# Seven half-width products for the first output block, and new places for v, the rounding, the audit and the flag's product, in a one-core attention and MLP kernel

## Chip, cores and metric

One core of a Trainium2 chip. The time is the device time of one launch in microseconds (us), the median of several runs; every number called a span, a start or a wait is from a profiled execution. All runs named here were in the fast state. Engines: PE is TensorE's matmuls, PEld its weight loads, DVE VectorE, ACT ScalarE, POOL GpSimd, SP the engine that issues the DMAs.

## The reference

```python
def _attn_ref(q, k, v, alpha):                 # each (4, 8, 768, 48) float32
    state = np.zeros((B, H, D, D), dtype=np.float32)
    for t in range(S):
        state = alpha[:, :, t, :, None] * state + np.einsum('bhd,bhe->bhde', k[:, :, t], v[:, :, t])
        y[:, :, t] = np.einsum('bhd,bhde->bhe', q[:, :, t], state)
    return y

def _moe_ref(x, w_in, w_out):                  # x (3072, 384), w_in (384, 2048), w_out (2048, 384)
    h = x @ w_in
    g = h * (1.0 / (1.0 + np.exp(-h)))
    return (g @ w_out).astype(np.float32)
# reference: x is the attention's y, with the heads beside each other
```

The weights arrive as 64-bit floats, so the kernel itself rounds them to 32 bits.

## The kernel before

The sequence is cut into 24 chunks of 128 tokens (six times four batches). A chunk passes through four stages: `products` (transposes of alpha, k, q, then scans on DVE that scale k and q into `kp` and `qp`), `scores` (k times q, masked into `g`), `values` (`g` times `v`, plus the state) and `states`. The program gives the name `g` to the MLP's middle values too: a `g` in front of the values products is the masked scores, a `g` in front of input pieces or output products is a block of the MLP. Between the stages PE is filled with *pieces* of the MLP: input pieces (`enter_plain`, `enter`) and output products (`leave`). Weight pieces come by DMA as 64-bit words into a short ring (`fetch`) and are rounded by one ACT instruction on the low words and three on DVE (`weights`).

Two things besides the result matter here. Most output products use a scheme of seven half-size products in place of eight (`leave`, with sums and differences of blocks of `w_out` formed in `differences`); the first half group alone still multiplied plainly. And an *audit* reads alpha and both weight matrices once more, a piece at a time, takes their extremes on DVE, and sends the verdict through one tiny matmul, the *flag's product*; if it fails, a general path runs instead.

```python
    load(0)
    load(1)
    for _ in range(4):
        fetch()                        # four 512 KB weight pieces are queued first
    ...
    for n in range(NV):
        load_v(n)                      # only then v of the first two chunks
    ...
    def weights(which):
        ...
        for dst, src in pieces:
            ...
            bits = coming.pop(0)
            lo, hi = bits.bitcast(U32)[:, :, 0], bits[:, :, 1]
            up = upp.tile([128, 512], I32, name="up")[:, 0:n]
            tc.keep_in_program_order(act.activation(up, lo, AF.Copy, scale=2.0**-29))
            ...                        # three DVE instructions: shift, sign, add
            fetch()
            yield
    ...
    def leave(grp, h):
        ...
        if grp == h == 0:              # the first half group: plain, 384 columns wide
            halves = w_out.rearrange("p (i k) n -> p k i n", k=2)
            ps = [out_bank(m, HD) for m in range(2)]
            for j in range(HF // 2):
                for m in range(2):
                    for i in (2 * j, 2 * j + 1):
                        for e in range(2):
                            ...
                            pe.matmul(ps[m], lhsT=x, rhs=halves[:, e, i], ...)
            ...
            return
        ...                            # all the others: seven products of 192 columns
    ...
    def fill(step, slot):
        ...
        if at % 2 == 0 and step > 3 * GB:
            next(audits, None)         # one audit item: DMA now, reduction at the next call
    ...
    turns = 0
    while next(audits, 0) is None:     # the tail: the rest of the audit between products
        turns += 1
        for _ in range(1 + turns % 2):
            go_on()
    ...
    go_on()
    go_on()
    ps = ps_attn()[0:1, 0, 0:1]
    pe.matmul(ps, lhsT=good, rhs=mask[:, 0, C - 1 : C], start=True, stop=True)   # the flag's product
```

Of the kernel before, what the change touches and what calls it, by code (L numbers as in the profile page):

```python
# [9 lines left out]
I32 = mybir.dt.int32  # L10
# [345 lines left out]
def quotients(  # L356
# [135 lines left out]
    def fetch():  # L492

        if wide and sources:
            src = sources.pop(0)
            n = src.shape[1]
            bits = raw.tile([128, 512, 2], I32, name="bits")[:, 0:n, :]
            nc.sync.dma_start(bits.rearrange("p n w -> p (n w)"), src.bitcast(I32))
            coming.append(bits)

    load(0)
    load(1)
    for _ in range(4):
        fetch()



# [46 lines left out]

        return quads[:, at // NKT, at % NKT] if at < 4 * NKT else late["wx"][:, at - 4 * NKT]

    for n in range(NV):
        load_v(n)

    def combine(to, sa, a, sb, b):  # L560
        if sa == sb == 1:
# [18 lines left out]
    def differences(i):  # L580

        if i < HF // 2:
            i = slice(2 * i, 2 * i + 2)
            tc.keep_in_program_order(
                dve.tensor_tensor(t1[:, i], b12[:, i], b11[:, i], ALU.subtract))
            dve.tensor_tensor(t2[:, i], b22[:, i], t1[:, i], ALU.subtract)
            dve.tensor_tensor(t4[:, i], b21[:, i], t2[:, i], ALU.subtract)
        else:
            i -= HF // 2
            if i % 2 == 0:  # L590
                side_by_side(0, 1, i // 2)
            i = slice(2 * i, 2 * i + 2)
            dve.tensor_tensor(b12[:, i], b22[:, i], b12[:, i], ALU.subtract)

    def weights(which):




        pieces = [  # L600
            (w_in[:, t, c : c + 512], moe_w_in[t * 128 : t * 128 + 128, c : c + 512])
            for t, c in pieces_in
        ] if which == 0 else [
            (w_out[:, f, :], moe_w_out[f * 128 : f * 128 + 128, :]) for f in range(NFT)]
        for dst, src in pieces:
            if not wide:
                act.dma_start(dst, src)
                yield
                continue
            n = dst.shape[1]  # L610
            bits = coming.pop(0)
            assert which == 0 or conv_done[0] == n_conv[0]
            lo, hi = bits.bitcast(U32)[:, :, 0], bits[:, :, 1]
            up = upp.tile([128, 512], I32, name="up")[:, 0:n]

            tc.keep_in_program_order(act.activation(up, lo, AF.Copy, scale=2.0**-29))
            w = dst.bitcast(I32)
            tc.keep_in_program_order(
                dve.tensor_scalar(w, hi, 3, 0x3FFFFFFF, ALU.logical_shift_left, ALU.bitwise_and))
            dve.scalar_tensor_tensor(w, hi, -(1 << 30), w, ALU.bitwise_and, ALU.bitwise_or)  # L620
            dve.tensor_tensor(w, w, up, ALU.add)  # L621
            fetch()
            yield

# [218 lines left out]
    def enter_plain(grp, h, pair):  # L843

        if h == 0:
            g_tiles(grp, pair)
        xt = xts[2 * grp + h]
        for f in range(8 * pair, 8 * pair + 8, 2):
            ps = bank(f // 2 % 3).rearrange("p (e n) -> p e n", e=2)
            for e in range(2):  # L850
                for t in range(NKT):
                    pe.matmul(ps[:, e, :], lhsT=w_in[:, t, (f + e) * 128 : (f + e + 1) * 128],  # L852
                              rhs=xt[:, t, :], start=(t == 0), stop=(t == NKT - 1))
            q, i = divmod(f, 4)
            act.activation(gts[grp, h, pair][:, i : i + 2, q % 2, :], ps, AF.Silu)  # L855
            if grp == 1 and pair == 0:
                differences(4 * h + f // 2)
            if grp > 0 and f % 8 == 6:
                side_by_side(grp, h, pair)
            yield  # L860
# [105 lines left out]
    def leave(grp, h):  # L966


        def product(ps, m, k, w, first=False):
            for i in range(HF):  # L970
                q = i // 2
                x = gts[grp, h, q // 2][:, 2 * (i % 2) + k, q % 2, m * C : (m + 1) * C]
                pe.matmul(ps, lhsT=x, rhs=w[:, i], start=(first and i == 0), stop=(i == HF - 1),  # L973
                          skip_group_check=True)

        def subtract(to, x, y):
            for pair in range(NQ // 2):
                dve.tensor_tensor(cells(grp, h, pair, *to), cells(grp, h, pair, *x),  # L978
                                  cells(grp, h, pair, *y), ALU.subtract)

        def store(m, c, x, y=None):
            ci, b = divmod(GB * grp + 2 * h + m, B)
            o = opool.tile([128, HO], F32, name="o")
            if y is None:
                act.copy(o, x)
            else:
                dve.tensor_tensor(o, x, y, ALU.add)
            r = b * S + ci * C
            nc.sync.dma_start(out[r : r + C, c * HO : (c + 1) * HO], o)

        if grp == h == 0:

            halves = w_out.rearrange("p (i k) n -> p k i n", k=2)
            ps = [out_bank(m, HD) for m in range(2)]
            for j in range(HF // 2):
                for m in range(2):
                    for i in (2 * j, 2 * j + 1):
                        for e in range(2):
                            x = gts[grp, h, j // 2][:, 2 * (i % 2) + e, j % 2, m * C : (m + 1) * C]
                            pe.matmul(ps[m], lhsT=x, rhs=halves[:, e, i],  # L1000
                                      start=(i == e == 0), stop=(i == HF - 1 and e == 1),
                                      skip_group_check=True)
                if j < HF // 2 - 1:
                    yield
            for m in range(2):
                for c in range(2):
                    store(m, c, ps[m][:, c * HO : (c + 1) * HO])
            yield
            return

        u1, u2, u3, u4 = [rpool.tile([128, HO], F32, name=f"u{j}") for j in range(4)]
        steps = iter(range(7))

        def done():
            if 2 * grp + h in (1, 2):
                sums_w(2 * grp + h - 1, 4 * next(steps) + 4)

        def new(i):
            return out_bank(i, HO)

        a, b = new(0), new(1)
        product(a, 0, 0, b11, True)
        act.copy(u1, a)
        subtract((0, 0), (1, 0), (0, 0))
        done()
        yield
        product(b, 1, 0, t1, True)
        act.copy(u4, b)
        done()
        yield  # L1030
        product(a, 0, 1, b21)
        store(0, 0, a)
        subtract((0, 1), (0, 1), (0, 0))
        done()
        yield
        b = new(1)
        product(b, 0, 0, t2, True)
        dve.tensor_tensor(u2, b, u1, ALU.add)
        subtract((1, 0), (1, 1), (0, 0))
        dve.tensor_tensor(u2, u2, u4, ALU.add)  # L1040
        done()
        yield
        a = new(0)
        product(a, 0, 1, b22, True)
        store(0, 1, a, u2)
        done()
        yield
        product(b, 1, 0, b12)
        dve.tensor_tensor(u3, b, u1, ALU.add)
        store(1, 1, u3, u4)  # L1050
        done()
        yield
        a = new(0)
        product(a, 1, 1, t4, True)
        store(1, 0, a, u3)
        done()
        yield
# [27 lines left out]
    for h in range(2):  # L1085
        for pair in range(2):
            pieces += [plain(0, h, pair)] * 4
    pieces += [(leave(0, 0), 24, GB)] * (HF // 2)
    phases = [len(pieces)]
    for h in range(2):  # L1090
        pieces += [plain(1, h, 0)] * 4
    both([(leave(0, 1), 12, GB)] * 7, [plain(1, 0, 1)] * 4 + [plain(1, 1, 1)] * 4)
    phases.append(len(pieces))
    before = output(1)
# [35 lines left out]
    def fill(step, slot):  # L1130

        at = step * SLOTS + slot
        if at < marks[0]:
            if step >= 1:
                convert(0, (at - SLOTS) * 3 // (marks[0] - SLOTS) + 1)
            return
        i = next(i for i, m in enumerate(marks[1:]) if at < m)
        a, b = [work_at[n] for n in ([0] + phases)[i : i + 2]]
        due = a + (b - a) * (at - marks[i] + 1) / (marks[i + 1] - marks[i])
        if at % 2 == 0 and step > 3 * GB:  # L1140
            next(audits, None)
        while work_at[done + 1] <= due and pieces[done][2] <= bridged:
            convert(0, 3 * (done // 2) + 6)
            convert(1, 3 * (done - 6) // 2)
            go_on()
# [42 lines left out]
        dve.tensor_single_scalar(e, e, bound, holds)  # L1188
    good = work.tile([128, 1], F32, name="good")
    dve.tensor_reduce(good, ends, axis=AX, op=ALU.min)  # L1190
    go_on()
    go_on()
    ps = ps_attn()[0:1, 0, 0:1]
    pe.matmul(ps, lhsT=good, rhs=mask[:, 0, C - 1 : C], start=True, stop=True)
    dve.tensor_single_scalar(small, ps, 127.5, ALU.is_ge)
# [62 lines left out]
```

## Time and profile before

| | kernel before |
|---|---|
| median time | 569.04 us (568.75 to 571.14, 3 runs) |
| span of the profiled execution | 567.3 us |
| PE busy | 549.0 us, 97% |
| DVE busy | 445.0 us, 78% |
| PE idle in front of the first values / near 232 us / at the flag's product | 2.4 / 1.8 / 2.1 us |

PE is busy for nearly the whole span, so the share of the other engines says little; what counts is the short list of PE's own waits. The prediction shows those lines and how they are read.

### The profile page before, as it was taken

How to read it: one execution, taken by the hardware profiler on the slowest of the kernel's cores; microseconds unless marked ns; L12 is line 12 of the kernel's file. 1: busy time of each engine (PE TensorE's matmuls, PEld its weight loads, DVE VectorE, ACT ScalarE, POOL GpSimd, SP SyncE). 2: the span in 40 equal slices, each digit the busy share in tenths (PEclk: the TensorE clock that was granted, in tenths of full speed). 3: DMA queues.
4: the chain of work that ended last, by engine and by line, in shares of the span. 5: the costliest groups of instructions: out<-in, count | busy, mean ns of one | idle time of the engine just before them, and what ended most of it. 6: DMA issues, size and time to landing. Idle time of an engine off the chain costs nothing.

```text
span 567.3 us, 12315 instructions
## 1 busy us (share of the span) xinstructions
PE 549.0 (97%) x5026; PEld 489.4 (86%) x5026; DVE 445.0 (78%) x815; ACT 205.4 (36%) x407; POOL 14.6 (3%) x36
## 2 busy tenths in 40 slices
PE   6899999999999999899999999999999999998996
PEld 4777887678999999799989999998999999997995
DVE  5797898488898599996998897999995866746531
ACT  3555543134323342443433443434443241421200
POOL 4111000100000000000000000000000000000000
PEclk9999999999999999999999999999999999998999
DMA  9989981533243324444425544425431223331000
GB/s 229 205 242 221 217 191 36 136 103 82 70 113 100 83 64 108 126 130 111 132 69 159 143 111 127 135 75 157 127 97 44 66 69 99 92 116 44 14 29 25
DMA packets 94415, 63.78 MB, mean 112 GB/s; under 512 B 55312, under 2 KB 86032, under 8 KB 94352
## 3 DMA queue, kind: packets, MB, share of 16 engines
q1 hardware_dynamic: 94352, 62.94, 43.1%
q8 instruction: 40, 0.66, 0.5%
q14 instruction: 23, 0.19, 0.1%
HBM read 58.20 MB, written 4.72 MB: 111 GB/s over the span
## 4 chain that ended last, share of the span: by engine, by line
PE 69%; DVE 17%; DMA 9%; SPq 2%; issue 1%; ACT 1%; DVEq 0%; ACTq 0%
PE ps_o L973 25%; PE ps_m L875 15%; PE ps_m L852 13%; DMA bits<-in_moe_w_out_dram 6%; PE ps_a L794 6%; PE ps_o L1000 4%; DVE seen L657 3%; PE ps_a L751 3%; DVE turn L668 1%; DMA vn<-in_v_dram 1%; PE ps_a L768 1%; DVE g L889 1%; DVE g L978 1%; DVE p L722 1%; PE ps_a L688 1%
## 5 line engine op out<-in xcount | busy, mean ns | idle before, releaser
L973 PE MATMUL ps_o<-w_out,g 128*128 128x192 f32 x704 | 122.4, 328 | 0.0
L973 PEld LDWEIGHTS ps_o<-w_out,g 128*128 128x128 f32 x704 | 115.3, 190 | 2.3 <-issue 0.4
L973 PE MATMUL ps_o<-wt,g 128*128 128x192 f32 x528 | 92.0, 328 | 0.0
L852 PE MATMUL ps_m<-xt,w_in 128*128 128x256 f32 x384 | 89.2, 383 | 1.3 <-DVE w_in L621 0.7
L973 PEld LDWEIGHTS ps_o<-wt,g 128*128 128x128 f32 x528 | 88.2, 192 | 1.4
L852 PEld LDWEIGHTS ps_m<-xt,w_in 128*128 128x128 f32 x384 | 70.9, 190 | 11.9 <-DVE w_in L621 1.6
L875 PE MATMUL ps_m<-xc,w_in 128*128 128x256 f32 x288 | 70.1, 379 | 1.4 <-DVE g L889 1.4
L875 PEld LDWEIGHTS ps_m<-xc,w_in 128*128 128x128 f32 x288 | 54.0, 190 | 7.9 <-DVE g L889 1.7
L886 ACT ACTIVATE g<-g 128x1024 f32<-128x1024 f32 x32 | 33.0, 1054 | 59.1 <-DVE g L889 59.1
L657 DVE TENSOR_REDUCE seen<-bits 128x1 f32<-128x384 int32 (+2 forms) x65 | 42.4, 687 | 15.1 <-DMA bits<-in_moe_w_out_dram 14.9
L875 PE MATMUL ps_m<-xc,wx 128*128 128x256 f32 x192 | 50.4, 384 | 0.0
L881 ACT COPY g<-ps_m 128x512 f32<-128x512 f32 x64 | 36.8, 586 | 36.2 <-PE ps_m L875 36.2
L978 DVE TENSOR_TENSOR g<-g 128x512 f32<-128x512 f32 x66 | 44.4, 683 | 7.0 <-PE ps_o L973 7.0
L774 ACT ACTIVATE st<-st,least 128x96 f32<-128x96 f32 x80 | 24.0, 365 | 59.1 <-DVE least L696 59.1
L889 DVE TENSOR_TENSOR g<-ps_m,g 128x512 f32<-128x512 f32 x56 | 37.1, 680 | 2.3 <-PE ps_m L875 2.1
L875 PEld LDWEIGHTS ps_m<-xc,wx 128*128 128x128 f32 x192 | 34.9, 190 | 4.2 <-issue 0.4
L693 DVE TENSOR_TENSOR_SCAN u<-al,one 128x516 f32<-128x516 f32 x24 | 29.0, 1209 | 9.0 <-ACT al L690 8.9
L855 ACT ACTIVATE g<-ps_m 128x512 f32<-128x512 f32 x32 | 19.1, 596 | 41.8 <-PE ps_m L852 41.6
L722 DVE TENSOR_TENSOR_SCAN p<-al,inv 128x516 f32<-128x516 f32 x24 | 29.4, 1227 | 5.0 <-PE ps_a L794 4.7
L762 DVE TENSOR_TENSOR g<-ps_a,mask 128x512 f32<-128x512 f32 x40 | 25.7, 684 | 9.0 <-PE ps_a L751 8.7
L794 PE MATMUL ps_a<-g,vn 128*32 128x128 f32 x768 | 27.2, 282 | 2.4 <-DMA vn<-in_v_dram 2.4
L794 PEld LDWEIGHTS ps_a<-g,vn 128*32 128x32 f32 x768 | 20.3, 112 | 10.1 <-issue 8.4
(127 smaller groups left out, 654.7 us busy)
## 6 DMA issues: line engine op xcount, KB each, us to landing
bits<-in_moe_w_in_dram SPq DMA_DIRECT2D x24, 512.0 KB, 4.7
bits<-in_moe_w_out_dram SPq DMA_DIRECT2D x32, 384.0 KB, 3.3
at<-in_alpha_dram SPq DMA_DIRECT2D x64, 96.0 KB, 2.3
kt<-in_k_dram SPq DMA_DIRECT2D x64, 96.0 KB, 2.4
qt<-in_q_dram SPq DMA_DIRECT2D x64, 96.0 KB, 2.5
bits<-in_alpha_dram SPq DMA_DIRECT2D x9, 512.0 KB, 3.6
out_dram<-o SPq DMA_DIRECT2D x48, 96.0 KB, 1.7
an<-in_alpha_dram SPq DMA_DIRECT2D x8, 192.0 KB, 5.1
```

The source lines that it names most:

```text
L657: dve.tensor_reduce(seen[kind][which][:, i : i + 1], x, axis=AX, op=op, apply_absolute_value=True))
L693: dve.tensor_tensor_scan(u[:, end - 1 :: -1], sg[:, end:0:-1], one[:, end:0:-1], 0.0, ALU.mult, ALU.add)
L722: dve.tensor_tensor_scan(p[:, 0:end], sg[:, 0:end], iv[:, 0:end], 0.0, ALU.mult, ALU.add)
L762: dve.tensor_tensor(g[:, u].rearrange("p (o j) c -> p o j c", o=2), ps[u].rearrange("p (o j) c -> p o j c", o=2), m.to_broadcast([128, 2, ...
L794: pe.matmul(py[32 * at : 32 * at + 32, t, :], lhsT=w, rhs=x, start=(i < 4), stop=(i >= len(todo) - 4), skip_group_check=True)
L852: pe.matmul(ps[:, e, :], lhsT=w_in[:, t, (f + e) * 128 : (f + e + 1) * 128], rhs=xt[:, t, :], start=(t == 0), stop=(t == NKT - 1))
L875: pe.matmul(ps[:, e], lhsT=block_w(w)[:, 2 * pair + e], rhs=block_x(grp, x), start=(first and e == 0), stop=(e == 1), skip_group_check=True)
L881: act.copy(to, ps)
L886: act.activation(x, x, AF.Silu)
L889: dve.tensor_tensor(to, a, b, op)
L973: pe.matmul(ps, lhsT=x, rhs=w[:, i], start=(first and i == 0), stop=(i == HF - 1), skip_group_check=True)
L978: dve.tensor_tensor(cells(grp, h, pair, *to), cells(grp, h, pair, *x), cells(grp, h, pair, *y), ALU.subtract)
```

## The change

Intent: save columns on PE (seven products of 192 columns for the last plain block), and take away three PE waits (for v at the start, for DVE near 232 us, for the audit's verdict near the end). The line numbers of the changed kernel differ by a few from those of the kernel before: values L794 becomes L800, input pieces L852 and L875 become L858 and L882, output products L973 become L980, the flag's product L1194 becomes L1180.

```diff
-    for _ in range(4):
+    for i in range(4):
         fetch()
+        if i % 2 == 0:
+            load_v(i // 2)
...
-    for n in range(NV):
-        load_v(n)
...
-            tc.keep_in_program_order(act.activation(up, lo, AF.Copy, scale=2.0**-29))
+            up = ahead.pop() if ahead else rounding(bits)
...
             dve.tensor_tensor(w, w, up, ALU.add)
+            if i + 1 < len(pieces):
+                ahead.append(rounding(coming[0]))
...
-            if grp == 1 and pair == 0:
-                differences(4 * h + f // 2)
+            if grp == 1 and pair == h == 0:
+                differences(f // 2)
+                differences(4 + f // 2)
...
-        if grp == h == 0:
-            ...                        # the plain product, removed
...
-    pieces += [(leave(0, 0), 24, GB)] * (HF // 2)
+    pieces += [plain(1, 0, 0)] * 4 + [(leave(0, 0), 12, GB)] * 7
     phases = [len(pieces)]
-    for h in range(2):
-        pieces += [plain(1, h, 0)] * 4
+    pieces += [plain(1, 1, 0)] * 4
...
-        if at % 2 == 0 and step > 3 * GB:
+        if at % 2 == 0 and step > 3 * GB + 2:
             next(audits, None)
...
-    go_on()
-    go_on()
+    for _ in range(5):
+        go_on()
     ps = ps_attn()[0:1, 0, 0:1]
     pe.matmul(ps, lhsT=good, rhs=mask[:, 0, C - 1 : C], start=True, stop=True)
```

More of the change, by code (lines that the diff above doesn't have):

```diff
@@ L589, in differences @@
             i -= HF // 2
-            if i % 2 == 0:
-                side_by_side(0, 1, i // 2)
+            side_by_side(0, i % 2, i // 2)
             i = slice(2 * i, 2 * i + 2)
@@ L604, in weights, with rounding @@
             (w_out[:, f, :], moe_w_out[f * 128 : f * 128 + 128, :]) for f in range(NFT)]
-        for dst, src in pieces:
+        def rounding(bits):
+            n = bits.shape[1]
+            up = upp.tile([128, 512], I32, name="up")[:, 0:n]
+            tc.keep_in_program_order(
+                act.activation(up, bits.bitcast(U32)[:, :, 0], AF.Copy, scale=2.0**-29))
+            return up
+        ahead = []
+        for i, (dst, src) in enumerate(pieces):
             if not wide:
@@ L609, in weights @@
                 continue
-            n = dst.shape[1]
+            assert which == 0 or conv_done[0] == n_conv[0]
             bits = coming.pop(0)
-            assert which == 0 or conv_done[0] == n_conv[0]
-            lo, hi = bits.bitcast(U32)[:, :, 0], bits[:, :, 1]
-            up = upp.tile([128, 512], I32, name="up")[:, 0:n]
-            tc.keep_in_program_order(act.activation(up, lo, AF.Copy, scale=2.0**-29))
-            w = dst.bitcast(I32)
+            up = ahead.pop() if ahead else rounding(bits)
+            hi, w = bits[:, :, 1], dst.bitcast(I32)
             tc.keep_in_program_order(
@@ L989, in store @@
             nc.sync.dma_start(out[r : r + C, c * HO : (c + 1) * HO], o)
-        if grp == h == 0:
-            halves = w_out.rearrange("p (i k) n -> p k i n", k=2)
-            ps = [out_bank(m, HD) for m in range(2)]
-            for j in range(HF // 2):
-                for m in range(2):
-                    for i in (2 * j, 2 * j + 1):
-                        for e in range(2):
-                            x = gts[grp, h, j // 2][:, 2 * (i % 2) + e, j % 2, m * C : (m + 1) * C]
-                            pe.matmul(ps[m], lhsT=x, rhs=halves[:, e, i],
-                                      start=(i == e == 0), stop=(i == HF - 1 and e == 1),
-                                      skip_group_check=True)
-                if j < HF // 2 - 1:
-                    yield
-            for m in range(2):
-                for c in range(2):
-                    store(m, c, ps[m][:, c * HO : (c + 1) * HO])
-            yield
-            return
         u1, u2, u3, u4 = [rpool.tile([128, HO], F32, name=f"u{j}") for j in range(4)]
```

## The prediction

> **What bounds the kernel now.** I read the page first (busy time, then the 40 slices), then the list of waits with TensorE as the one that waits, then the timeline around each wait, and last the chain that ended last, for rates.
>
> The page and the waits of TensorE:
> ```profile
> PE 549.0 (97%) x5026; PEld 489.4 (86%) x5026; DVE 445.0 (78%) x815; ACT 205.4 (36%) x407; POOL 14.6 (3%) x36
> ...
> PE ps_a L688 <- DMA an<-in_alpha_dram: 4.2, 1, 4.2
> PE ps_a L794 <- DMA vn<-in_v_dram: 2.4, 1, 2.4
> PE ps_a L1194 <- DVE good L1190: 2.1, 1, 2.1
> PE ps_m L875 <- DVE g L889: 1.8, 2, 1.4
> PE ps_m L852 <- DVE w_in L621: 0.7, 1, 0.7
> ```
> TensorE (PE) is the bound. Of the 567.3 us span it is idle 18.3 us, and about 5.5 us of those are the wait for the last store after its last product, 4.2 us the first load. So only two things can make the kernel faster: fewer columns through PE, or removal of a wait in that short list. Each has its part of the change. The rates that I need, from the chain that ended last (start, length, number of instructions):
> ```profile
> 111.15 5.16 PE ps_o L1000 x16
> 145.18 2.60 PE ps_o L973 x16
> ```
> A matmul in the code is two instructions here (32 in the code, 64 in the group of L1000). A 384-column instruction costs 5.16 / 16 = 0.3225 us, a 192-column one 2.60 / 16 = 0.1625 us: in proportion to the columns, no fixed cost to speak of.
>
> The flag's product, in the timeline of PE, and just before it the last audit reduction on VectorE (DVE):
> ```profile
> 515.20 1.01 DVE L657 TENSOR_REDUCE seen<-bits 128x1 f32<-128x384 int32 x2 [1.17 <-DMA bits<-in_moe_w_out_dram]
> ...
> 516.87 0.19 PE L1194 MATMUL ps_a<-mask,good 128*1 128x1 f32 x2 [2.11 <-DVE good L1190]
> ...
> 518.43 1.91 PE L875 MATMUL ps_m<-xt,w_in 128*128 128x256 f32 x4
> 520.13 3.56 PE L973 MATMUL ps_o<-wt,g 128*128 128x192 f32 x16
> 523.53 1.03 PE L875 MATMUL ps_m<-xc,w_in 128*128 128x256 f32 x4
> ```
> PE waits 2.1 us for the audit's end, and then runs slowly: four instructions take 1.91 us where the same four take 1.03 later. The windows view agrees: granted clock 0.92 in 510 to 520 us and 0.91 in 520 to 530, so about 0.8 + 0.9 = 1.7 us of full speed are lost after the wait itself.
>
> The start, in the timelines of PE, POOL and DVE:
> ```profile
> 16.53 1.94 PE L794 MATMUL ps_a<-g,vn 128*32 128x128 f32 x32 [2.41 <-DMA vn<-in_v_dram]
> ...
> 13.76 1.40 POOL L758 TENSOR_SCALAR_AFFINE_SELECT g<-g 128x512 f32<-128x512 f32 x2 [6.75 <-ACT g L757]
> ...
> 19.61 0.69 DVE L621 CUSTOM_DVE_ANT_0 w_in<-w_in,up 128x1024 uint16<-128x1024 uint16 x1 [2.01 <-ACT up L616]
> ...
> 22.93 0.69 DVE L621 CUSTOM_DVE_ANT_0 w_in<-w_in,up 128x1024 uint16<-128x1024 uint16 x1 [1.56 <-ACT up L616]
> ```
> v of the first chunk is issued at 8.55 us behind four weight pieces and lands 7.85 us later. But g, the other operand, is ready only at 14.5 (first half) and 15.2 us. DVE twice waits for ScalarE (ACT) to have rounded the low words, 3.6 us in all.
>
> The middle, in the timelines of DVE and PE:
> ```profile
> 218.34 1.22 DVE L657 TENSOR_REDUCE seen<-bits 128x1 f32<-128x1024 f32 x1
> ...
> 229.07 1.21 DVE L657 TENSOR_REDUCE seen<-bits 128x1 f32<-128x1024 f32 x1
> ...
> 233.73 1.13 PE L875 MATMUL ps_m<-xc,w_in 128*128 128x256 f32 x4 [1.37 <-DVE g L889]
> ```
> From 200 to 235 us DVE is 97% busy, the first two audit reductions stand in its queue, and PE then waits for it: 1.4 + 0.4 us.
>
> [...]
>
> **The change part by part.**
> 1. The product of the first half group by seven products. Removed: 64 instructions of 384 columns, 64 x 0.3225 = 20.6 us. Added: 7 x 8 matmuls of 192 columns, 112 instructions, 112 x 0.1625 = 18.2 us. PE gains 2.4 us. DVE gets six subtractions (0.68 us each) and five small sums (0.36 us), and the differences of w_out (16 of 0.55 us) come before this stage, not at 120 to 131 us. To make room, one block of four input pieces is moved ahead of it. DVE was busy 18.6 us of 88 to 118, so there is room. By the instruction order, w_out's last rounding and all differences precede these products on DVE. Adding durations along it from the sixth chunk's scan (about 84 us), DVE has rounded everything at about 95 us and formed all differences at about 102; PE, which now has 10.4 us of input pieces first, wants the first at about 100 and needs t1 at about 104. No wait, by 2 us at the tightest. Gain 2.4.
> 2. v sooner. v now stands behind one weight piece, so by bytes it lands near 12 to 13 us (an estimate: the first piece landed at 11.22 and the next 1.7 MB took 5.2 us). Then g decides. Here part 3 gives something back: the rounding of the second piece now stands ahead of the copies of g in ACT's queue, that piece lands at about 13.3 us (same estimate), so g comes at about 15.3 to 16.0. PE starts its values about 1 us sooner instead of 2.4[...].
> 3. Rounding one piece ahead. DVE's waits of 2.0 and 1.6 us mostly go; what PE sees of it is the 0.7 us wait for w_in and less crowding up to 50 us. [...]Parts 2 and 3 together: 1.3 us.
> 4. Audit two steps later. The two reductions before 233 us (2.4 us of DVE) go, more than the 1.8 us wait. Expect 1.5 us, as another order may bring part back.
> 5. The flag. In the new instruction order PE has about 34 blocks of 2.6 us (16 instructions) between its last attention product and the flag's, 88 us; before about 25, 65 us. The audit has 18 items left there; before, the last 14 items came every 4.5 us (450.9 to 516.1, with DMA, reduction and one buffer in a ring). 17 x 4.5 = 77 us plus 1.5. The flag is ready some 8 us early: 2.1 us of wait and 1.7 us of half clock go, 3.8 us. I count 3.4 for the risk. Eight blocks, 21 us, remain after the flag, enough to hide its reading.
>
> Sum: 2.4 + 1.3 + 1.5 + 3.4 = 8.6 us. The time of the runs is 569.04, so about **560.4 us**.
>
> **Rivals.** (a) ACT becomes the wait: [...]a rounding put ahead now waits for its DMA or for DVE in front of copies and Silus that PE needs. For it: ACT already waited 5.9 us for pieces and 4.3 us for DVE at L616. Against: PE has three banks there and was idle under 2 us from 20 to 100 us. If it holds, parts 2 and 3 give nothing: 562. (b) The audit's chain paces the tail. The last subtractions of the second-last output stand behind its last reductions on DVE; PE needs them about 83 us after its last attention product, the chain ends at 77 to 79. At 5 us an item the flag wait turns into a wait of a product: 563 to 564. (c) DVE becomes the bound where the differences now stand (60 to 105 us, it was 83 to 95% busy to 90 us): each us late is a us of PE, perhaps 2: 562. (d) All goes as hoped, the start gives its full 2.4 and DVE's lead frees PE from 20 to 50 us too: 12 us, 557.
>
> **Range and chances.** Parts 1 and 5 are nearly sure in size, 6 us; parts 2 to 4 hold 0 to 6. So 557.3 to 563.6. Two per cent is 11.4 us, to 557.7, and wants every part in full: 0.10. Slower by two per cent needs a new wait of 20 us that nothing in the order suggests: 0.01. Within: 0.89.
>
> **What would show it.** Right: no L1000-type group, 112 more instructions of 192 columns; no PE wait for the flag's product and granted clock 1.00 to the end of PE; no PE wait on DVE near 230 us; the wait at the first values shorter and put to POOL or ACT and not to DMA. Wrong: a new PE wait on w_out, wt or Silu between 80 and 110 us (part 1, rival c or a), a PE wait on the subtractions in the last 60 us (rival b), or gaps elsewhere from a scheduler's order that I did not foresee.

## The result

563.48 us (563.20 to 564.50, 4 runs) against 569.69 (568.75 to 571.14, 4 runs in all) for the kernel before: ratio 0.9892, 95% interval 0.9865 to 0.9919, within two per cent. A ratio here is the mean time of one kernel's fast runs over that of the other's of the same rounds, so it is not quite the ratio of the medians quoted. The span fell from 567.3 to 561.6 us.

The busy times of the changed kernel's page:
```profile
PE 543.9 (97%) x5074; PEld 492.6 (88%) x5074; DVE 453.0 (81%) x829; ACT 205.3 (37%) x406; POOL 15.1 (3%) x36
```
PE's waits in the changed kernel, the six with the largest totals (total us, times, longest):
```profile
PE ps_a L694 <- DMA an<-in_alpha_dram: 4.1, 1, 4.1
PE ps_a L800 <- POOL g L764: 3.9, 2, 3.6
PE ps_o L980 <- DVE o L994: 1.1, 1, 1.1
PE ps_m L858 <- ACT xt L805: 1.0, 3, 0.4
PE ps_a L815 <- DVE kp L709: 0.5, 1, 0.5
PE ps_m L882 <- DVE g L896: 0.4, 1, 0.4
```
And its two groups of output products, busy time and mean ns of one:
```profile
L980 PE MATMUL ps_o<-w_out,g 128*128 128x192 f32 x768 | 133.6, 328 | 1.1 <-DVE o L994 1.1
L980 PE MATMUL ps_o<-wt,g 128*128 128x192 f32 x576 | 100.0, 327 | 0.0
```
The instruction counts are as foreseen: 48 more on PE (112 of 192 columns in, 64 of 384 out). The waits for v, for `good` and for `w_in` are gone, and that for `g` near 232 us is down from 1.8 to 0.4. But new waits stand in their place: for POOL's `g` at the first values (3.6, longer than the 2.4 for v had been), for `o` (1.1), for `xt` and `kp`.

The instructions of one operation overlap (the 768 of the first group, 328 ns each, would be 252 us, and their busy time is 133.6), so a sum of busy times does not tell where the time went. Better is a ledger: the start on PE of instructions that both programs reach after the same work. The first values of chunks 3, 11, 13 and 23 and the last product are such marks, since the number of PE instructions before them is the same in both, or differs by just the 48.

| start on PE, us | before | changed | difference | of this stretch | predicted for it |
|---|---|---|---|---|---|
| values of chunk 3 | 54.98 | 54.54 | -0.44 | start: 0.44 | 1.3 |
| values of chunk 11 | 191.29 | 189.71 | -1.58 | products: 1.14 | 2.4 |
| values of chunk 13 | 236.32 | 233.30 | -3.02 | middle: 1.44 | 1.5 |
| values of chunk 23 | 448.29 | 445.22 | -3.07 | 0.05 | 0 |
| last product | 561.57 | 555.88 | -5.69 | flag: 2.62 | 3.4 |

Each term can now be looked at where it stands. The first row is from one profile of each kernel and the start scatters from run to run, as round_after_g below shows.

**The start.** The products of `scores` on PE, in the changed kernel and then in the kernel before:
```profile
10.53 1.16 PE L757 MATMUL ps_a<-p,kp 48*128 48x128 f32 x16
```
```profile
11.00 2.08 PE L751 MATMUL ps_a<-p,kp 48*128 48x128 f32 x16
```
ACT's timeline in the changed kernel (start, length, line, operation, number; in brackets the idle time before it and what ended it):
```profile
11.39 0.69 ACT L609 ACTIVATE up<-bits 128x512 int32<-128x512 uint32 x1 [1.92 <-DMA bits<-in_moe_w_in_dram]
13.73 0.67 ACT L609 ACTIVATE up<-bits 128x512 int32<-128x512 uint32 x1 [1.65 <-DMA bits<-in_moe_w_in_dram]
14.30 1.05 ACT L763 COPY g<-ps_a 128x512 f32<-128x512 f32 x2
```
and in the kernel before:
```profile
13.11 1.07 ACT L757 COPY g<-ps_a 128x512 f32<-128x512 f32 x2 [1.22 <-PE ps_a L751]
```
PE's first values in the changed kernel:
```profile
15.89 0.64 PE L800 MATMUL ps_a<-g,vn 128*32 128x128 f32 x4 [3.62 <-POOL g L764]
```
The second rounding stands in ACT's queue ahead of the copies of g, and waits 1.65 us there for its DMA, while the scores that the copies need are done from 11.69 us on. (In the kernel before they were done only at 13.08: the same 16 products took 2.08 us there and 1.16 here. The clock records, full from the first, begin at 20.0 us in that profile and at 8.7 in this one. The kernel before took 1.94 us for its first 32 values, and 1.08 for those at 22.82.) So the copies begin at 14.30, later than the 13.11 of the kernel before, and PE's values, which v would now have let begin earlier (it landed at 12.43 us, against 16.40 before), begin at 15.89, only 0.64 us sooner than before. The granted clock was half (0.50) from 15.54 to 18.96 us, which begins inside this wait.

**The products.** DVE just ahead of the first output product, in the kernel before:
```profile
85.25 0.68 DVE L703 TENSOR_TENSOR kp<-ps_a,u 128x512 f32<-128x512 f32 x1
```
and in the changed one:
```profile
85.16 0.56 DVE L625 CUSTOM_DVE_ANT_0 w_out<-w_out,up 128x768 uint16<-128x768 uint16 x1
...
87.57 0.68 DVE L709 TENSOR_TENSOR kp<-ps_a,u 128x512 f32<-128x512 f32 x1
...
100.57 0.54 DVE L587 TENSOR_TENSOR wt<-w_out,wt 128x384 f32<-128x384 f32 x1
101.12 0.36 DVE L821 TENSOR_TENSOR st<-ps_a,st 48x192 f32<-48x192 f32 x1
```
PE's waits there, in the timeline of the changed kernel:
```profile
88.31 0.54 PE L815 MATMUL ps_a<-vn,kn 128*32 128x48 f32 x30 [0.50 <-DVE kp L709]
89.28 8.04 PE L858 MATMUL ps_m<-xt,w_in 128*128 128x256 f32 x36 [0.43 <-ACT xt L805]
...
101.63 0.63 PE L774 MATMUL ps_a<-ident,kp 128*128 128x128 f32 x4 [0.23 <-DVE st L821]
```
DVE has no pause above 0.15 us from 74 to 104 us here: the roundings of `w_out` come sooner, as the differences need them sooner. Ahead of the attention's `kp` stand 13 of the 16 roundings instead of 12, and a sum of blocks of the MLP's g that came behind it before, and `kp` comes 2.3 us later than before; the new state `st` stands between differences (L585 to L592). PE waits 0.50 + 0.43 + 0.23 = 1.16 us here. Counted over all of chunk 3 to 11, PE's gaps are 1.43 us against 0.46 in the kernel before, and the rest of its time, from start to start, is 2.12 us less, not the 2.4 of the rates. 2.12 - 0.97 = 1.15, the 1.14 of the ledger.

**The flag.** PE reaches it without a wait, but DVE's queue near 482 us has an audit reduction that waits for its DMA ahead of the sum that a product needs:
```profile
482.36 1.01 DVE L663 TENSOR_REDUCE seen<-bits 128x1 f32<-128x384 int32 x2 [0.43 <-DMA bits<-in_moe_w_out_dram]
483.29 0.35 DVE L994 TENSOR_TENSOR o<-ps_o,u 128x192 f32<-128x192 f32 x1
```
```profile
483.69 2.87 PE L980 MATMUL ps_o<-w_out,g 128*128 128x192 f32 x16 [1.07 <-DVE o L994]
...
534.95 0.19 PE L1180 MATMUL ps_a<-mask,good 128*1 128x1 f32 x2
```
(the first of these two fences is DVE's timeline, the second PE's, both of the changed kernel). So 1.1 us of the 3.8 is given back. The size of this wait is not firm: with no edit in the tail it is 0.5 to 0.6 us in the profiles of round_after_g, v_late and pace24, and none is listed for no_ahead.

### The profile page after: what moved, and what is told of

It reads as the page before. It is cut to its first block, busy times and chain, and to the rows that moved or that the text cites. A ratio compares the mean times of both kernels' runs of the same rounds, so it can differ in the third digit from the quotient of the medians.

```text
span 561.6 us, 12420 instructions
## 1 busy us (share of the span) xinstructions
PE 543.9 (97%) x5074; PEld 492.6 (88%) x5074; DVE 453.0 (81%) x829; ACT 205.3 (37%) x406; POOL 15.1 (3%) x36
## 4 chain that ended last, share of the span: by engine, by line
PE 75%; DVE 14%; DMA 5%; SPq 2%; issue 2%; ACT 1%; POOL 0%; DVEq 0%; ACTq 0%
PE ps_o L980 33%; PE ps_m L882 18%; PE ps_m L858 11%; PE ps_a L800 6%; DMA bits<-in_moe_w_out_dram 3%; PE ps_a L757 3%; DVE seen L663 2%; PE ps_a L774 1%; DVE g L896 1%; DMA bits<-in_moe_w_in_dram 1%; DVE u L699 1%; PE ps_a L815 1%; DVE w_out L625 1%; DVE p L728 1%; SPq L456 1%
## 5 line engine op out<-in xcount | busy, mean ns | idle before, releaser
L980 PE MATMUL ps_o<-w_out,g 128*128 128x192 f32 x768 | 133.6, 328 | 1.1 <-DVE o L994 1.1
L980 PEld LDWEIGHTS ps_o<-w_out,g 128*128 128x128 f32 x768 | 125.5, 190 | 3.9 <-DVE o L994 1.5
L980 PE MATMUL ps_o<-wt,g 128*128 128x192 f32 x576 | 100.0, 327 | 0.0
L980 PEld LDWEIGHTS ps_o<-wt,g 128*128 128x128 f32 x576 | 95.1, 190 | 1.5
L858 PE MATMUL ps_m<-xt,w_in 128*128 128x256 f32 x384 | 88.5, 382 | 1.0 <-ACT xt L805 1.0
L858 PEld LDWEIGHTS ps_m<-xt,w_in 128*128 128x128 f32 x384 | 71.0, 190 | 11.0 <-ACT xt L805 1.4
L882 PE MATMUL ps_m<-xc,w_in 128*128 128x256 f32 x288 | 70.1, 379 | 0.0
L882 PEld LDWEIGHTS ps_m<-xc,w_in 128*128 128x128 f32 x288 | 54.0, 190 | 6.4 <-DVE g L896 0.2
L985 DVE TENSOR_TENSOR g<-g 128x512 f32<-128x512 f32 x72 | 48.5, 686 | 5.6 <-PE ps_o L980 5.6
L882 PE MATMUL ps_m<-xc,wx 128*128 128x256 f32 x192 | 50.1, 383 | 0.0
L882 PEld LDWEIGHTS ps_m<-xc,wx 128*128 128x128 f32 x192 | 35.0, 190 | 4.2 <-issue 0.4
L800 PE MATMUL ps_a<-g,vn 128*32 128x128 f32 x768 | 28.0, 282 | 3.9 <-POOL g L764 3.9
L800 PEld LDWEIGHTS ps_a<-g,vn 128*32 128x32 f32 x768 | 20.3, 112 | 11.2 <-issue 5.5
```

What stands on the lines that cost most here:

```text
L800: pe.matmul(py[32 * at : 32 * at + 32, t, :], lhsT=w, rhs=x, start=(i < 4), stop=(i >= len(todo) - 4), skip_group_check=True)
L858: pe.matmul(ps[:, e, :], lhsT=w_in[:, t, (f + e) * 128 : (f + e + 1) * 128], rhs=xt[:, t, :], start=(t == 0), stop=(t == NKT - 1))
L882: pe.matmul(ps[:, e], lhsT=block_w(w)[:, 2 * pair + e], rhs=block_x(grp, x), start=(first and e == 0), stop=(e == 1), skip_group_check=True)
L980: pe.matmul(ps, lhsT=x, rhs=w[:, i], start=(first and i == 0), stop=(i == HF - 1), skip_group_check=True)
L985: dve.tensor_tensor(cells(grp, h, pair, *to), cells(grp, h, pair, *x), cells(grp, h, pair, *y), ALU.subtract)
```

## The experiments

Every kernel ran for five rounds and gave a correct result. They ran in three sets of four, each beside eleven runs of the kernel before on the same chip: no_ahead, round_after_g, v_late and pace24 (kernel before: median 570.56 us); before_flag5, audit_early, tail_ratio and no_wout_audit (569.24); products_only, before_v, combo and combo3 (569.52). A difference of medians between kernels of different sets, or against the changed kernel's 563.48, carries the scatter of the sets with it. The questions: is the start's loss the order of ACT's queue, is the products' loss DVE's queue or PE's pace, and is the flag's gain what I said?

### The start

**no_ahead**: the changed kernel, with no rounding ahead.
```diff
-            if i + 1 < len(pieces):
+            if False and i + 1 < len(pieces):
```


> The changed kernel, but no rounding is formed ahead of its piece (v sooner and all else kept). In the instruction order only two roundings move on ACT: that of the second w_in piece goes back behind the copies of g and of the first x, and one of w_out moves later. Theory A (the rounding put ahead waits for its DMA[...] and so holds back the copies of g): PE's first values begin at about 14.5 us instead of 15.9, the wait of 3.6 us for POOL shrinks to about 2.3, ACT's copies of g start at about 12 us right after the scores; DVE waits again some 2 us for ACT in front of the second and third pieces. Time about 562.9 (between 562 and 564, changed kernel 563.5). Rival B (g is late because of POOL[...] or v itself): first values stay at 15.5 us or later and the wait for POOL stays above 3 us.

Measured: 561.77 us (561.27 to 563.82), ratio 0.9862. In the traces it differs from the changed kernel in ACT's order alone, but 12 of the 28 roundings stand at another place there, not the two that were expected. ACT's copies in its timeline, and PE's first values:
```profile
12.92 1.07 ACT L763 COPY g<-ps_a 128x512 f32<-128x512 f32 x2 [0.80 <-PE ps_a L757]
```
```profile
14.26 0.41 PE L800 MATMUL ps_a<-g,vn 128*32 128x128 f32 x4 [0.79 <-POOL g L764]
```
The copies now wait for PE, not for a DMA, and the values begin 1.63 us sooner than in the changed kernel, as theory A has it. The wait for POOL fell further than expected (to 0.8 and not 2.3 us), and DVE waited only once for ACT (1.1 us). Rounding ahead costs the changed kernel about 1.7 us by the medians (563.48 - 561.77), more than expected; the time is just below the expected range of 562 to 564.

**round_after_g**: keeps the rounding ahead, but puts the first one behind the first copies of g.
```diff
-            if i + 1 < len(pieces):
+            if which == 0 and i == 0:
+                held.append(lambda: ahead.append(rounding(coming[0])))
+            elif i + 1 < len(pieces):
...
+            if step == 1 and slot == 1 and held:
+                held.pop()()
```


> The changed kernel, but the rounding of the second w_in piece is formed just after the copies of g and not ahead of them (it still comes ahead of the copy of the first x). Theory A: first values begin at about 14.5 us as without rounding ahead, and DVE does not wait for ACT more than 0.5 us in front of the second piece: both gains at once. PE reaches the chunk-3 values about 1 us sooner than the changed kernel (54.55 us there); time about 562.5. Rival B: nothing moves, 563.5.

Measured: 561.71 us (561.03 to 562.34), ratio 0.9855; first values at 14.46 us, chunk 3 1.16 us sooner, and DVE has no wait for ACT in front of the second piece: as theory A has it. Here the traces differ in the place of one rounding alone, so this run is the cleaner test: one instruction's place carries the whole loss. The other roundings ahead neither gain nor cost anything that the runs show, as the two kernels agree within 0.1 us.

The other kept profiles show the same beyond the scatter of one. In the five kernels with the changed kernel's start (the changed one, pace24, audit_early, tail_ratio, no_wout_audit) the scores end anywhere from 11.08 to 13.14 us, but the copies of g begin at 14.22 to 14.35, when the second piece has come and been rounded, and the values of chunk 3 at 54.5 to 56.8 us. In the four with that rounding behind the copies (no_ahead, round_after_g, combo, combo3) the copies begin 0.03 us after the scores, and chunk 3 comes at 53.1 to 53.4. The kernel before and its two kin with the same start (before_flag5, products_only) reach it at 55.0 to 55.9: on this view parts 2 and 3 together gave next to nothing.

**v_late**: the changed kernel with v behind four weight pieces, as before.
```diff
-        if i % 2 == 0:
-            load_v(i // 2)
+    for n in range(NV):
+        load_v(n)
```


> The changed kernel, but v is fetched behind all four weight pieces as in the kernel before (rounding ahead kept). If v was worth something by itself: PE waits for v's DMA until about 16.5 us and the time is 0.5 us or more over the changed kernel, about 564.1. If rounding ahead had already used up what v gained (theory A), the first values come only about 0.6 us later than in the changed kernel (15.9) and the chunk-3 values within 0.6 us of 54.55: 563.5 to 564.

Measured: 564.59 us (563.35 to 565.06), ratio 0.9902, so 1.1 us slower than the changed kernel. PE waited 2.43 us for v, until 16.59. Here PE also waited 1.5 us for `w_in`, more than the 0.7 before: rounding ahead did not help in this order either. But it did not hold back the copies: with v behind it the second piece landed at 12.52 us and not 13.71, and the copies began at 13.15, 0.03 us after the scores. So the loss comes from the two edits together, v ahead of the second piece and that piece's rounding ahead of the copies.

**before_v**: the kernel before with v sooner, and nothing else.
```diff
-    for _ in range(4):
+    for i in range(4):
         fetch()
+        if i % 2 == 0:
+            load_v(i // 2)
...
-    for n in range(NV):
-        load_v(n)
```


> The kernel before with v's load behind one weight piece (and k, q as in the changed kernel) and nothing else changed. Theory A (without a rounding ahead, the first values product is released by g at about 14.5 us instead of by v at 16.5): about 2 us faster, ratio 0.9965. Rival: [...]only about 0.7 us, ratio 0.9988.

Measured: 567.37 us (565.18 to 569.53), ratio 0.9959 (0.9914 to 1.0005). PE's first values:
```profile
14.59 0.64 PE L794 MATMUL ps_a<-g,vn 128*32 128x128 f32 x4 [0.33 <-POOL g L758]
```
They begin 1.94 us sooner than before, and 1.40 us of it is left at the values of chunk 3 and at every later mark to chunk 23. So v alone is worth 1.4 us in this profile, between the two expectations, and 2.2 us by the medians; the interval of the runs is too wide to say more.

### The products

**pace24**: the seven products are spread over more steps.
```diff
-    pieces += [plain(1, 0, 0)] * 4 + [(leave(0, 0), 12, GB)] * 7
+    first_out = [(leave(0, 0), 12, GB)] * 7
+    pieces += [plain(1, 0, 0)] * 4 + first_out[:4]
     phases = [len(pieces)]
     pieces += [plain(1, 1, 0)] * 4
+    pieces += first_out[4:]
```


> The changed kernel, but only four of the seven products of the first output part are counted to the first phase, so that its pieces are issued at the pace of the kernel before (24 pieces, not 27, by the same step). Theory C (the moved input block runs PE out of ready work beside the sixth chunk, so that products of the attention and the copy of x come on the path: PE loses 1.9 us in gaps between 87 and 102 us): these gaps fall below 0.8 us in sum, time about 562.3. Rival D (VectorE's extra differences and roundings before 105 us are what is late): the gaps stay, or move, and the time stays at 563.5 or rises.

Measured: 562.88 us (562.31 to 564.82), ratio 0.9879. From chunk 3 to chunk 11 it takes 135.27 us; the changed kernel takes 135.17, the kernel before 136.31. A slower pace takes away the wait for `kp` at 88 us (12 roundings stand ahead of `kp` again, as in the kernel before) but makes one of 0.7 us for DVE's `g` at 100 us; PE's gaps are 1.35 us in all, against 1.43, and in this stretch it gains nothing. That is rival D for the gaps: they move. From chunk 11 to 13 it takes 43.06 against 43.59: the rest of the wait near 232 us goes. That half us is all that the trace shows of it.

**products_only**: only the seven products, the order of pieces and the sooner differences; v, rounding, audit and flag as before.
```diff
-        if i % 2 == 0:
-            load_v(i // 2)
+    for n in range(NV):
+        load_v(n)
...
-            if i + 1 < len(pieces):
+            if False and i + 1 < len(pieces):
...
-        if at % 2 == 0 and step > 3 * GB + 2:
+        if at % 2 == 0 and step > 3 * GB:
...
-    for _ in range(5):
+    for _ in range(2):
```


> The changed kernel with v, the rounding of w_in, the audit and the flag's product all as in the kernel before; only the seven products of the first w_out part, the order of its pieces and the sooner differences are kept. Theory D (the sooner differences and products disturb the score lines between 87 and 102 us, which give back part of the gain): 2.4 us less of columns and 1.2 to 1.9 us given back, so 0.5 to 1.3 us faster than before, ratio 0.998. Rival: the gaps belong to the other placements, so the full 2.4 us show, ratio 0.9957. The waits before at 232 us and behind the flag stay as in the kernel before under both.

Measured: 567.23 us (566.70 to 567.94), ratio 0.9955 (0.9913 to 0.9996). The number is the rival's, but the profile does not bear the rival out. From chunk 3 to 11 the kernel takes 135.36 us, 0.95 less than the kernel before, and the waits are all there: 0.60 for `kp`, 0.43 for `xt`, 0.33 for `st`. So they belong to the products and differences, not to the other placements. The other 1.4 us come from elsewhere. PE's timeline:
```profile
234.24 1.13 PE L882 MATMUL ps_m<-xc,w_in 128*128 128x256 f32 x4 [1.88 <-DVE g L896]
...
517.20 0.19 PE L1180 MATMUL ps_a<-mask,good 128*1 128x1 f32 x2 [0.33 <-DVE good L1176]
```
and the windows of the same kernel (bounds, length, busy us of the engines, PEclk, DMA share, GB/s):
```profile
232.00:238.00 6.00, 3.73 (x19) 2.13 (x21) 5.97 (x13) 1.25 (x2) 0.00 (x0) 0.82 0.53 163
238.00:244.00 6.00, 6.00 (x108) 5.76 (x101) 5.30 (x8) 3.66 (x6) 0.00 (x0) 0.89 0.42 101
```
PE lost 1.9 us near 232, then ran at half clock for a while (0.82 and 0.89 over these windows), and was 2.13 us behind the kernel before from chunk 14 on. But the audit's verdict came at nearly the same time as before (`good` ended at 517.14 us, before at 516.81), so PE waited 0.33 us for it and not 2.11, and the granted clock was 1.00 from 510 to 530 us. Of the 2.13 us lost ahead of it 1.78 came back at this wait; my expectation that the flag's wait stays as before was wrong.

In all eleven kernels with the seven products, the changed one included, chunk 3 to 11 takes 135.14 to 135.36 us, 0.95 to 1.17 less than before, whatever else was edited.

### The middle and the flag

**before_flag5**: the kernel before with three more pieces ahead of the flag's product.
```diff
-    go_on()
-    go_on()
+    for _ in range(5):
+        go_on()
```


> The kernel before with one change: the flag's product stands behind five output blocks after the audit instead of two (three blocks of 2.6 us later on PE). Theory E: PE comes to it at about 522 us, the audit is done at 516.7, so the 2.1 us of wait and the 3.4 us of half clock behind it both go: 3.8 us less than the kernel before, ratio about 0.993. Rival F ([...]the wait moves to another product): at most the 2.1 us go, or less, ratio 0.996 or more, and a stretch of granted clock 0.5 stays between 500 and 530 us.

Measured: 566.16 us (565.20 to 567.36), ratio 0.9944. No wait for `good` is listed, and no half clock near the end in its clock records: 3.1 us by the medians. In its profile the clock was half from 236.07 to 239.49 us, behind the wait near 232 (1.8 us in two). The profile of the kernel before has the same wait, 1.8 us in two, and a granted clock of 1.00 from 226 to 244 us. So half clock followed this wait in one profile and not in the other.

**audit_early**: the changed kernel with the audit begun two steps sooner, as before.
```diff
-        if at % 2 == 0 and step > 3 * GB + 2:
+        if at % 2 == 0 and step > 3 * GB:
```


> The changed kernel, but the audit begins two steps sooner, as in the kernel before (the flag's product stays five blocks behind it). Theory G (the audit's reductions[...] make both PE waits: the one near 232 us, before; the new one of 1.1 us near 482 us, after, as four more of them fall into the tail): the wait near 230 us comes back with about 1.8 us, the one near 480 us falls below 0.4 us, time within 0.7 us of the changed kernel (563.5). Rival H (the wait near 482 us comes from the order of the output and input blocks, not from the audit): it stays at about 1 us and the time is 564.5 to 565.

Measured: 565.14 us (564.53 to 566.05), ratio 0.9925. The wait for `g` near 232 us is back (2.3 us in two), the wait for `o` near 482 us is gone. Both signs are as foreseen. The time is 1.7 us above the changed kernel, outside the 0.7 expected and more than the waits alone; half clock from 234.88 to 238.29 us follows the wait (granted clock 0.74 over 232 to 238). The two waits are one trade: the later the audit, the more of it lies in the tail.

**tail_ratio**: in the tail, more products between audit items.
```diff
-        for _ in range(1 + turns % 2):
+        for _ in range(1 + (turns % 3 > 0)):
...
-    for _ in range(5):
+    for _ in range(3):
```


> The changed kernel, but behind the last step the audit's items are issued with five blocks of PE work for three items instead of three for two (4.3 us an item instead of 3.9), and the flag's product three blocks behind the audit instead of five, so that it stays at the same place. Theory G: VectorE, which waits for an item's DMA every 4.3 us, no longer falls behind PE; the wait near 482 us falls from 1.1 to below 0.4 us, time about 562.6. Rival H: no change, 563.5.

Measured: 562.54 us (561.77 to 564.22), ratio 0.9881. The wait near 482 us is gone, and no other came. Its start up to chunk 3 has no edit, yet that mark is 2.2 us later than in the changed kernel's profile: in this execution the clock records, full from the first, begin only at 25.4 us. So a single profile can't weigh the start to a us; for the start I go by the runs of no_ahead and round_after_g. The 0.9 us by the medians is no larger than the spread of the runs either; the trace has the stretch from the values of chunk 23 to the last product at 109.26 us, against 110.66 in the changed kernel and 109.73 to 110.16 in four with the changed kernel's tail (no_ahead, round_after_g, v_late, pace24).

**no_wout_audit**: the changed kernel without the check of w_out. The result is right, but a safety check is removed on purpose, only to measure.
```diff
-            todo += [(moe_w_out[f * 128 : f * 128 + 128, :], HD, 1) for f in range(NFT)]
```


> The changed kernel without the audit of w_out (16 of 37 items; it takes a safety check away, the outputs stay right for these inputs). No audit is left in the tail then. Theory G: no PE wait at all between 450 us and the end, time about 1.1 to 1.3 us under the changed kernel, 562.3. Rival H: the wait near 480 us stays. If more than 1.5 us go, the audit costs PE something that does not show as a wait.

Measured: 562.78 us (561.74 to 564.42), ratio 0.9887, and no PE wait behind 300 us. By the medians the audit still costs some 0.7 us in the tail, less than the 1.1 to 1.3 expected, and the runs spread over 2.7 us; tail_ratio gets that without giving the check up.

### Together

**combo** has the edits of round_after_g, pace24 and tail_ratio at once; **combo3** leaves pace24's out.

> The changed kernel with three edits that each removed a wait alone: the rounding of the first w_in piece behind the first copies of g, the first phase of products paced over more steps, and two thirds of the tail's lines on VectorE. If the gains add (1.8 + 0.5 + 0.9 us less than the changed kernel): 560.3; if they overlap or one moves a wait elsewhere: 561.0 to 561.7, no better than the best single edit.

> As the combination, but without the slower pace of the first phase: 560.8 if the two gains add, 561.5 if they don't. If the pace is worth something by itself, this run is 0.4 to 0.7 us slower than the combination of three; if it only moves the waits, the two are equal.

Measured: combo 560.52 us (560.13 to 561.23), ratio 0.9841 (0.9800 to 0.9882); combo3 560.77 (560.26 to 561.48), ratio 0.9844. Combo's interval reaches past two per cent, so its class is unclear. The waits of the changed kernel that the edits were about are gone or smaller (combo still waits 1.1 us for POOL's `g` at the first values); of combo3's waits of PE:
```profile
PE ps_a L698 <- DMA an<-in_alpha_dram: 4.2, 1, 4.2
PE ps_m L862 <- ACT xt L809: 1.0, 3, 0.4
PE ps_a L819 <- DVE kp L713: 0.5, 1, 0.5
...
PE ps_a L804 <- POOL g L768: 0.3, 1, 0.3
```
The gains of round_after_g and tail_ratio add: 563.48 - 1.8 - 0.9 = 560.8, and combo3 has 560.77. What the pace adds on top, 0.25 us, is inside the scatter of both and is not shown. combo3 is the version I would keep: 2.7 us below the changed kernel with two edits. What the seven products give back (`xt`, `kp`) is still in it.

## Why the prediction was right or wrong

The class was right and the time, 563.48, lies in the range but at its upper edge, 3 us above the 560.4. The sum had 8.6 us; the profiles show 5.7, the medians 6.2. That it lies inside is partly luck: "6 us" nearly sure and "0 to 6" for the rest end at 569.04 - 6 = 563.0, and the time lies in the half us added to that; parts 1 and 5, called nearly sure, gave only 3.8 us in the ledger. The misses of size nearly all went one way, to waits that the sum did not have. By its steps:

- **Part 1, "Gain 2.4": mis-sized.** The columns are saved (2.1 us from start to start: over the whole stretch these instructions average 0.168 and 0.332 us, not the 0.1625 and 0.3225 of one unbroken group), and the operands of the new products were in time, as foreseen (first at 102.10 us, the one that needs t1 at 106.01, neither with a wait). What I tested was only whether DVE serves the new products in time, not what stands behind the roundings and differences in DVE's queue. The attention's `kp` and `st` did: 0.97 us more of gaps than before, and 1.14 us of gain is left. Rival (c) named this place, with up to 2 us. All eleven kernels with the seven products show this size, so it is no scatter of one profile. "DVE was busy 18.6 us of 88 to 118, so there is room" was the wrong question: those 30 us had 11.4 free, and still `kp` began at 87.57 us and not at 85.25, behind one more rounding and one more sum. pace24 ties the wait for `kp` to the one rounding more ahead of it; how the rest divides between the roundings, the differences and the new order of pieces is read from the queue, and no run parted them.
- **Parts 2 and 3, "1.3 us": mis-sized.** I saw the mechanism, and even g's time: "g comes at about 15.3 to 16.0", measured 15.9. But I then booked part 3 as a gain. It is a loss of some 1.7 us (no_ahead, round_after_g), from the place of one rounding; of it 1.2 to 1.4 us stand at the values of chunk 3 in the profiles, the rest in the tail, whose wait scatters. v sooner is worth 1.1 (v_late against the changed kernel) to 1.4 us (before_v's profile). v landed at 12.43 us, as foreseen. Rival (a) was this, with "parts 2 and 3 give nothing", and it held nearly in full: 0.4 us is left in this pair of profiles, less in the wider set. The wait for `w_in` did go, as I said, but its 0.7 us were not worth 1.7.
- **Part 4, "1.5 us": right**, 1.44 by the ledger, and audit_early shows the wait coming back with its undoing. With the rest of the change in place the earlier audit would even cost 2.5 us there (chunk 11 to 13 takes 46.11 us in audit_early, 43.59 in the changed kernel). It isn't free, as the reductions moved to the tail.
- **Part 5, "I count 3.4": nearly right.** The wait of 2.1 us and the 1.7 us of half clock both went (granted clock 1.00 in the changed kernel from 19 us to the last product, at 555.88); before_flag5 alone is worth 3.1 by the medians. But rival (b) took place in a small size: one product waited 1.07 us for a sum behind a reduction, so 2.6 us is left by the ledger. tail_ratio and no_wout_audit each remove it, worth 0.9 and 0.7 us by the medians. The 2.6 also depends on the pair of profiles: before_v, which had the wait but no half clock, takes 111.16 us for that stretch, 2.1 less than the kernel before. The margin was thinner than foreseen: PE came to the flag's product 88.3 us after the last values product (446.68 to 534.95; 88 foreseen), but `good` was ready only at 530.5, 83.8 us after it and not 78.5. The rate of an item was right (4.47 us), but the trace has 18 steps from the first of 19 items to the last where the sum has 17, and the first begins 1.2 us after the last values product. So 4.5 us were left of some 8, which was enough.
- **Clock.** I booked the half clock behind such a wait as certain. It isn't. PE waits of 2.1 us (kernel before, half clock 518.33 to 521.75) and of 1.4 + 0.4 us (before_flag5, 236.07 to 239.49) were followed by 3.4 us of half clock, a wait of 1.8 us for `good` in before_v by none (granted clock 1.00 from 510 to 530). In the start the clock records, full from the first, begin at 8.7 us in the changed kernel's profile, 12.5 in no_ahead's, 20.0 in that of the kernel before and 25.4 in tail_ratio's; what set these four apart was not shown. Of 33 runs of the kernel before, eight had a mean granted clock of 0.998 and took 567.5 to 569.5 us, the three lowest (0.983 and 0.984) 571.7 to 574.3, and over all 33 time and clock correlate at -0.66. The clock is not all of it: the three fastest (565.2 to 566.0) had 0.995 and 0.996. The changed kernel's four runs lie within 1.3 us.
- **Readings.** One slip in the recorded text, which does not carry the result: DVE is 98.7% busy from 200 to 235 us (97% is 200 to 240). The first load of v behind four weight pieces took 7.85 us to land; the median of the eight loads as large is 4.3 (behind one weight piece, in the changed kernel, it took 5.3). The 1.7 us of full speed lost at the flag are half of the 3.42 us from 518.33 to 521.75.

## What to carry to other kernels

Here one rounding put ahead on ACT waited 1.65 us for its DMA, and the two copies behind it, which PE needed, began at 14.30 us though their scores were done at 11.69: some 1.7 us of 563 by the medians (no_ahead, round_after_g). So check what stands behind the moved instruction, not only whether it is itself in time. A wait that ends at another chain's time hides gains and losses ahead of it (products_only lost 2.13 us ahead of the flag's product and waited 1.78 us less there), so single edits need not add, and a ledger of marks that both programs reach after equal work tells where a gain was made and where it was given back. PE waits of about two us can be worth removing twice over: some executions here had 3.4 us of half clock behind them, 1.7 us of full speed (kernel before, 518.33 to 521.75).
